# Unread products in TensorE's gaps, and the last expert's rows gathered earlier, in a kernel of attention and two expert layers

## The chip, the core and the metric

One core of a Trainium2 chip. TensorE (PE) multiplies matrices into PSUM; its weights go in by a load of their own (PEld). VectorE (DVE) and ScalarE (ACT) do elementwise work and read PSUM; GpSimd (POOL) works on SBUF alone and issues the gathers and scatters (indirect DMAs); SyncE (SP) issues the plain loads. The metric is the device time of the whole launch in microseconds (us).

## What is computed

Three stages, each on the output of the one before; numpy, cut:

```
# 1: attention, 4 batches, 8 heads, 768 positions, 64 wide: window of 96 and 8 global keys
x = attention(q, k, v).reshape(3072, 512)
# 2: first expert layer: tokens with x @ w_skip > 0, each to its best of 8 experts
e_idx = argmax(xc @ w_gate); gate = softmax(xc @ w_gate)[e_idx]
out[do_compute] = xc + gate * (relu(xc @ w1[e]) @ w2[e])        # w1 512x1024, w2 1024x512
# 3: second expert layer: pairs (token, expert) in order of falling logit;
#    a token goes to the first expert with room, 384 tokens for each of 8
out[mask_e] = relu(x[mask_e] @ w1[e]) @ w2[e]
```

## The kernel before, in words

**Precision.** The experts' products run in fp32r with both operands split in a high and a low part, three products for each (`P3`). A weight chunk of 128x1024 is loaded into `wr`, ACT writes its high part `wh`, and POOL (four pieces of 256 columns) or DVE (one piece) the low part `wl`. `W_.pump()` loads and splits the next chunk if its turn has come; `need(chunk)` splits up to that chunk. Four `wr` buffers are in use: a load waits until the chunk four places earlier is split.

**First layer.** After attention, the routing (`route1`) makes lists of rows (`gid`, `sid`). While it does so, `ww(n)` multiplies parts of two experts' w2 with the next layer's gate; it runs up to the end of that stage. A loop over overflow blocks follows, which here runs zero times; every engine passes its exit. Then come the units, one for each expert, of up to 208 rows: `x_load` gathers the rows (`xg`), `x_stream` transposes them on PE (bank `pt`) into `xh` on ACT and `xl` on DVE, `mm1` makes `ph`, which ACT turns into h (relu) and DVE into its low half, and `mm2_turned` makes `py`. Between the sixth and the seventh expert an extra unit (`extra`, `extra_rest`) handles one overflow block of 128 rows: two halves of `ph<-wh,th`, four transposes for each half, 24 products `py<-wh,th`. The two last experts run `mm1` first and their second products later; they are read with tiles named `py` of 128 and 80 rows, while the second layer's routing goes on.

**Second layer.** The routing (`routing`, `phase`) finds for one expert after the other the threshold that fills it: seven rounds of comparing (`gm` on DVE), counting (`pr<-oh,gm` on PE), deciding (`fl`, `wt`). Then `slots` makes the row list: `ttb`, `part`, `mp` are its small products. Eight units of 384 rows follow; the next expert's routing runs among their products.

**Order.** The program is written by one planner that keeps a model clock for each engine (`ck.at`, `ck.ready`, constants such as 0.19 us between engines). Streams (rows to transpose, routing, the extra unit) hand out steps; `hook` takes a step ahead of a product if the model says that its inputs are ready, `wait_for` steps streams until a condition holds. What stands in the program then runs in that order on each engine. `ck.late` is what the model adds to a gather's 2.7 us until it has landed.

Of the kernel before, what the change touches and what calls it, by code (L numbers as in the profile page):

```python
# [7 lines left out]
F32 = mybir.dt.float32  # L8
# [155 lines left out]
def tile_attn_moe_moe(ctx: ExitStack, tc: tile.TileContext, q, k, v, n_global, n_local,  # L164
                      w_skip, w_gate, w1, w2, w2_gate, w21, w22, out):
    nc = Chip(tc.nc)
# [366 lines left out]
    WWT, WWN = 1, (2, 5)  # L533
    T_GAP, T_SP, T_EPS, T_W, T_P, T_L, T_F, X_B, T_H, T_M, LEAN, T_G, DIRECT, CUT = 0, 0.65, 0.1, 0, 8, 1, 0.3, 3, -4, 0, 2, 1, 13, 16
    T_LOW = 0.7
    ck.late = 2.0
    W_ = Weights()

# [208 lines left out]
        return product  # L747

    ww_todo, ww_turns, ww_k = [], [], [0]

    def ww(n):
        for _ in range(n):
            late = list(ww_turns)
            ww_turns.clear()
            if ww_k[0] < 2 * FC:
                ww_todo.append(ww_step(ww_k[0]))
                ww_k[0] += 1
            if len(ww_todo) > 1 or ww_k[0] == 2 * FC and ww_todo:
                ww_todo.pop(0)()
            for f in late:  # L760
                f()
# [107 lines left out]
    def x_load(U_, nb):  # L869
        U_.xs, U_.xt, U_.at, U_.tb = [], {}, ck.at["pe"], 0  # L870
        ids = U_.ids()
        for tb in range(nb):
            n = U_.n[tb]
            if U_.third:
                xg = ff.tile([128, Dm + E], F32, name=f"xt{tb}", bufs=1)
            elif tb < 2:
                xg = xp.tile([128, Dm + E], F32, name=f"xg{tb}", bufs=2)
            else:
                xg = ff.tile([128, Dm], F32, name=f"xg{tb}", bufs=2)
            gather(xg[:n, :U_.src.shape[1]], U_.src, ids[:n, tb:tb + 1])  # L880
            U_.xs.append(xg)
# [71 lines left out]
    nc.vector.memset(cnt, 2.0)  # L953
    over_rest = over_list(rp, ps, "x", 1.0, gidx, sidx, gwtx, "pP", 5)
    while ww_k[0] < 2 * FC:
        ww(1)
    over_rest()
    while ww_todo or ww_turns:
        ww(1)
    att.close()  # L960
    n_units = nc.values_load(novi[0:1, E:E + 1], min_val=0, max_val=N // 128)
    with tc.For_i(0, n_units, 1):
# [189 lines left out]
    def need(chunk):  # L1152
        while chunk not in W_.parts:
            b4 = W_.split
            W_.pump(True)
            assert W_.split > b4
# [38 lines left out]
            else:  # L1195
                return

    def wait_for(over):
        while not over():
            t = min(s_.when() for s_ in order()) + T_F  # L1200
            s_ = next(s_ for s_ in order() if s_.when() <= t)
            if unit_no[0] < 0 and s_.kind == "main":
                first_ = min((o for o in order() if o.kind != "main"), key=lambda o: o.when(), default=None)
                if first_ and first_.when() < s_.when() + T_M:
                    s_ = first_
            s_.step()

    lows = []
# [339 lines left out]
    def extra(U_, finish):  # L1548

        if U_.g == NE - 1:  # L1550
            X_.xt = {}
            X_.xs = [fx_.tile([128, Dm + E], F32, name="xgx")]
            X_.xh, X_.xl = (fx_.tile([128, KC, 128], F32R, name=n) for n in ("th0", "tl0"))
            gather(X_.xs[0], xd, gidx)
            start("extra", x_stream(X_))
        if U_.g != NE + 1:
            return False
        wait_for(lambda: X_.tb == 1)
        W_.done, W_.f = NE, 0
        need(NE * NCH + 3)  # L1560
        hs_ = []
        for half in range(2):
            ph = fps.tile([128, 512], F32, name="ph", bufs=2)
            xx = (X_.xh, X_.xl)
            for i, (a, b_) in enumerate(P3):
                for c in range(KC):
                    w_ = W_.parts[NE * NCH + c][b_]
                    hook(w_)
                    nc.tensor.matmul(ph, xx[a][:, c, :128], w_[:, half * 512:(half + 1) * 512],
                                     start=i == 0 and c == 0, stop=c == KC - 1 and i == 2)  # L1570
            h2 = ff.tile([128, 2, wide_h], F32, name="h2", bufs=3)
            for i in range(2):
                hs_.append(h2[:, i])
                nc.scalar.activation(hs_[-1], ph[:, i * wide_h:(i + 1) * wide_h], AF.Relu)
            if half == 0:
                finish()
            W_.pump()
            W_.pump()
        start("extra", extra_rest(hs_))
        return True  # L1580

    def extra_rest(hs_):
        hT = []
        for half in range(2):
            yield "pt", hs_[2 * half:2 * half + 2]
            flush()
            p = turns()
            for c in range(4):
                nc.tensor.transpose(p[:, c], hs_[2 * half + c // 2][:, c % 2 * 128:(c % 2 + 1) * 128], ident)
            th = fx_.tile([128, 4, 128], F32R, name=f"th{half}")  # L1590
            tl_ = fx_.tile([128, 4, 128], F32R, name=f"tl{half}")
            nc.scalar.activation(th, p, AF.Copy)
            nc.vector.tensor_tensor(tl_, p, th.bitcast(F32), op=OP.subtract)
            hT.append((th, tl_))
            X_.turned += 1
        X_.y = [fps.tile([128, Dm], F32, name="py2")]
        for c in range(FC):
            need(NE * NCH + 4 + c // 2)
            ww = W_.parts[NE * NCH + 4 + c // 2]
            for i, (a, b_) in enumerate(P3):  # L1600
                yield "pe", [hT[c // 4][a], ww[b_]]
                nc.tensor.matmul(X_.y[0], hT[c // 4][a][:, c % 4], ww[b_][:, (c % 2) * Dm:(c % 2 + 1) * Dm],
                                 start=c == 0 and i == 0, stop=c == FC - 1 and i == 2)
            W_.free = 4 * NE + (c + 1) // 2
            W_.pump()
        epi1(X_, [])
        yield from gate_rows(X_, 1)
# [16 lines left out]
    for tb in range(HI):  # L1624
        x_low(units1[0], tb)
    need(NCH - 3)
    run_units(units1, HI, epi1, (), between)


# [233 lines left out]
    for U_ in units1[NE:]:  # L1863
# [10 lines left out]
            W_.pump()  # L1874
        for tb in range(HI):
            row_late(U_, tb)
    wait_for(lambda: 0 in result)
    f1x.close()
    ff = ctx.enter_context(tc.tile_pool(name="ff", bufs=2))
    width = wide_h = CAP  # L1880
# [18 lines left out]
    def last_blocks(U_, steps):  # L1899

        need(U_.g * NCH + NCH - 1)
        for tb in range(NH):
            for _, f, h in steps:
                ww = W_.parts[U_.g * NCH + 4 + f // 2]
                for i, (a, b_) in enumerate(P3):
                    te(U_.y[tb], h[a][:, tb * 128:(tb + 1) * 128], ww[b_][:, (f % 2) * Dm:(f % 2 + 1) * Dm],
                       start=False, stop=f == FC - 1 and i == 2)
            o = ff.tile([128, Dm], F32, name=f"o{tb}", bufs=1)
            nc.scalar.activation(o[:, :Dm // 2], U_.y[tb][:, :Dm // 2], AF.Copy)
            dv.tensor_copy(o[:, Dm // 2:], U_.y[tb][:, Dm // 2:])  # L1910
            put(U_, tb, o)

    units2 = []
# [18 lines left out]
    def split_next():  # L1932
        need(W_.order[W_.split])

    split_next()
    ck.late = 0
    units2[0].banks = ("pt", "py1", "py2")
    units2[0].load()
    ck.late = 2.0
    split_next()  # L1940
    split_next()
    wait_for(lambda: units2[0].tb == NH)
    split_next()
    W_.on_pool = range(NCH)

    run_units(units2, NH, epi2, by_block=last_blocks)
# [34 lines left out]
```

## Time and profile before

| | us |
|---|---|
| runs | 794.14, 795.55, 795.29, median 795.29 |
| the profiled execution, its own time | 796.18 |
| its span | 794.4 |
| PE busy | 744.9 (94%) |
| DVE, ACT, POOL busy | 528.7, 402.4, 461.6 |

Times of rows count from the start of the span. A row of the timeline reads: start, duration, engine, line, operation, output <- inputs, shapes, how many merged, and in brackets the engine's idle time ahead of it and what ended it. Helpers record every operation, so that all stand at L125. Products are pipelined: the spacing of two rows tells more than their durations. [...]

### The profile page before, as it was taken

How to read it: one execution, taken by the hardware profiler on the slowest of the kernel's cores; microseconds unless marked ns; L12 is line 12 of the kernel's file. 1: busy time of each engine (PE TensorE's matmuls, PEld its weight loads, DVE VectorE, ACT ScalarE, POOL GpSimd, SP SyncE). 2: the span in 40 equal slices, each digit the busy share in tenths (PEclk: the TensorE clock that was granted, in tenths of full speed). 3: DMA queues.
4: the chain of work that ended last, by engine and by line, in shares of the span. 5: the costliest groups of instructions: out<-in, count | busy, mean ns of one | idle time of the engine just before them, and what ended most of it. 6: DMA issues, size and time to landing. Idle time of an engine off the chain costs nothing.

```text
span 794.4 us, 17216 instructions
## 1 busy us (share of the span) xinstructions
PE 744.9 (94%) x5807; PEld 626.9 (79%) x5807; DVE 528.7 (67%) x1953; ACT 402.4 (51%) x934; POOL 461.6 (58%) x807
## 2 busy tenths in 40 slices
PE   6999999999979899999889949999999999999997
PEld 4887777777659899999778627888887888789986
DVE  5987979979456676666643576878787787832111
ACT  5887787887546555555642213343442435345221
POOL 4664556755123474665552635696876859599711
PEclk9999999999989999999989977999999999999999
DMA  8686888988617766668650061536263636466210
GB/s 188 173 209 177 228 225 197 249 200 220 190 48 264 211 200 210 218 218 250 198 198 7 18 212 62 162 104 225 96 213 124 181 125 192 135 184 186 80 41 40
DMA packets 143833, 132.21 MB, mean 166 GB/s; under 512 B 65427, under 2 KB 110739, under 8 KB 143744
## 3 DMA queue, kind: packets, MB, share of 16 engines
q1 hardware_dynamic: 135360, 111.19, 48.9%
q0 software_dynamic: 6784, 19.51, 7.1%
q8 instruction: 47, 0.77, 0.4%
q10 hardware_dynamic: 1600, 0.39, 0.2%
q14 instruction: 42, 0.34, 0.1%
HBM read 108.80 MB, written 22.79 MB: 166 GB/s over the span
## 4 chain that ended last, share of the span: by engine, by line
PE 42%; POOL 11%; issue 8%; DVE 5%; ACT 2%; DMA 2%; POOLq 0%; DVEq 0%; ACTq 0%
PE ph L125 19%; PE py L125 18%; POOL wl L125 8%; PE pr L125 4%; PE pt L125 2%; DVE wl L125 1%; POOL out_dram L125 1%; ACT wh L125 1%; POOL xg L125 1%; DVE py L125 1%; DMA xg<-xd,gid 1%; DMA wr<-in_moe_w_dram 1%; DMA xg<-x2d,ids 0%; DVE h L125 0%; ACT h L125 0%
## 5 line engine op out<-in xcount | busy, mean ns | idle before, releaser
L125 POOL TENSOR_TENSOR wl<-wr,wh 128x256 fp32r<-128x256 f32 x340 | 246.0, 756 | 77.2 <-ACT wh L125 76.5
L125 ACT ACTIVATE wh<-wr 128x1024 fp32r<-128x1024 f32 (+1 forms) x148 | 141.4, 985 | 41.3 <-DMA wr<-in_moe_w_dram 23.3
L125 PE MATMUL py<-wh,h 128*128 128x512 f32 (+1 forms) x448 | 156.6, 405 | 0.0
L125 ACT ACTIVATE h<-ph 128x208 fp32r<-128x208 f32 (+2 forms) x132 | 54.8, 416 | 189.5 <-PE ph L125 173.4
L125 POOL TENSOR_SCALAR pb<-pb,st 128x232 f32<-128x232 f32 (+1 forms) x192 | 83.9, 458 | 73.3 <-ACT pb L125 25.2
L125 DVE SCALAR_TENSOR_TENSOR h<-ph,h 128x208 fp32r<-128x208 f32 (+1 forms) x128 | 58.9, 460 | 101.4 <-ACT h L125 101.0
L125 ACT ACTIVATE pb<-sb,st 128x232 f32<-128x232 f32 (+1 forms) x192 | 113.8, 663 | 10.2 <-DVE st L125 9.6
L125 PE MATMUL ph<-xh,wh 128*128 128x208 f32 (+1 forms) x512 | 103.5, 317 | 4.1 <-DVE h L125 2.2
L125 PE MATMUL ph<-xh,wl 128*128 128x208 f32 (+1 forms) x512 | 103.5, 316 | 0.0
L125 PE MATMUL ph<-xl,wh 128*128 128x208 f32 (+1 forms) x512 | 101.2, 316 | 0.0
L125 PEld LDWEIGHTS ph<-xh,wh 128*128 128x128 f32 x512 | 84.8, 194 | 11.0 <-DVE h L125 2.9
L125 PEld LDWEIGHTS py<-wh,h 128*128 128x128 f32 (+1 forms) x448 | 81.4, 186 | 14.1
L125 PE MATMUL py<-wl,h 128*128 128x512 f32 (+1 forms) x224 | 90.6, 405 | 0.0
L125 PEld LDWEIGHTS ph<-xl,wh 128*128 128x128 f32 x512 | 81.5, 195 | 1.4 <-issue 1.0
L125 PEld LDWEIGHTS ph<-xh,wl 128*128 128x128 f32 x512 | 81.7, 195 | 0.6 <-issue 0.4
L125 DVE TENSOR_TENSOR wl<-wr,wh 128x1024 fp32r<-128x1024 f32 x51 | 64.7, 1276 | 20.2 <-ACT wh L125 20.2
L125 DVE CUSTOM_DVE_ANT_0 sb<-pS,bias 128x232 f32<-128x232 f32 (+1 forms) x192 | 61.4, 374 | 7.9 <-PE pS L125 6.5
L125 DVE COPY pts<-pP 116x512 f32<-116x512 f32 (+1 forms) x96 | 60.6, 672 | 7.5 <-PE pP L125 7.1
L125 POOL DMA_INDIRECT xg<-x2d,ids x24 | 23.3, 970 | 49.4 <-DVE py L125 25.4
L125 PE MATMUL pP<-ident,pb 128*116 128x128 f32 (+1 forms) x384 | 51.1, 276 | 0.0
L125 PE MATMUL pS<-kt,qt 64*128 64x232 f32 (+1 forms) x384 | 49.5, 377 | 1.0 <-ACT pb L125 1.0
L125 PE MATMUL py<-h,wh 128*128 128x416 f32 x192 | 47.9, 363 | 2.4 <-DVE h L125 2.4
(460 smaller groups left out, 1243.4 us busy)
## 6 DMA issues: line engine op xcount, KB each, us to landing
wr<-in_moe_w_dram SPq DMA_DIRECT2D x136, 512.0 KB
xd<-xs SPq DMA_DIRECT2D x32, 192.0 KB
x2d<-xs SPq DMA_DIRECT2D x32, 192.0 KB
kraw<-in_k_dram SPq DMA_DIRECT2D x30, 192.0 KB
qraw<-in_q_dram SPq DMA_DIRECT2D x30, 192.0 KB
vw<-in_v_dram SPq DMA_DIRECT2D x32, 160.0 KB
vw<-in_v_dram SPq DMA_DIRECT2D x32, 120.0 KB
xT<-in_moe_w_dram SPq DMA_DIRECT2D x1, 1536.0 KB
```

The lines of the kernel that those rows point to most:

```text
L125: r = f(*a, **k)
```

## The change

Unread products ("fillers": 128 x 256 columns of the constants `ones` and `tri`, into a PSUM bank that nobody reads) are put on PE in three places: in the last calls of `ww` and ahead of the loop (9, 6 and 6), behind the first unit's transposes (8), and, by `wait_for(..., True)`, up to 0.15 us ahead of each step that the planner expects between the layers (106). The eighth expert's rows (`units1[E - 1]`) are gathered as the extra unit begins, and two pumps move ahead of the extra unit's products; the stream that transposes those rows starts in `extra_rest`. For the second layer's first gathers the planner's `ck.late` is 1.7 where it was 0. The last output blocks are copied by ACT alone.

```
@@ -533,6 +533,7 @@
     WWT, WWN = 1, (2, 5)
     T_GAP, T_SP, T_EPS, T_W, T_P, T_L, T_F, X_B, T_H, T_M, LEAN, T_G, DIRECT, CUT = 0, 0.65, 0.1, 0, 8, 1, 0.3, 3, -4, 0, 2, 1, 13, 16
     T_LOW = 0.7
+    T_U = 0.15
     ck.late = 2.0
     W_ = Weights()
 
@@ -747,14 +748,23 @@
         return product
 
     ww_todo, ww_turns, ww_k = [], [], [0]
-
-    def ww(n):
+    wide_one = ones[:, None, :].to_broadcast([128, 2, 128])
+
+    def keep(n):
+
+        if n:
+            p = ps.tile([128, 512], F32, name="pO")
+            for _ in range(n):
+                nc.tensor.matmul(p[:, :256].rearrange("p (a n) -> p a n", a=2), tri, wide_one, start=True, stop=True)
+
+    def ww(n, unread=0):
         for _ in range(n):
             late = list(ww_turns)
             ww_turns.clear()
             if ww_k[0] < 2 * FC:
                 ww_todo.append(ww_step(ww_k[0]))
                 ww_k[0] += 1
+            keep(unread)
             if len(ww_todo) > 1 or ww_k[0] == 2 * FC and ww_todo:
                 ww_todo.pop(0)()
             for f in late:
@@ -953,10 +963,11 @@
     nc.vector.memset(cnt, 2.0)
     over_rest = over_list(rp, ps, "x", 1.0, gidx, sidx, gwtx, "pP", 5)
     while ww_k[0] < 2 * FC:
-        ww(1)
+        ww(1, 9 if ww_k[0] == 2 * FC - 1 else 0)
     over_rest()
     while ww_todo or ww_turns:
-        ww(1)
+        ww(1, 6 if ww_turns else 0)
+    keep(6)
     att.close()
     n_units = nc.values_load(novi[0:1, E:E + 1], min_val=0, max_val=N // 128)
     with tc.For_i(0, n_units, 1):
@@ -1195,7 +1206,14 @@
             else:
                 return
 
-    def wait_for(over):
+    def warm(until):
+
+        if ck.at["pe"] + 0.11 <= until:
+            p = fps.tile([128, 512], F32, name="ph", bufs=2)
+            while ck.at["pe"] + 0.11 <= until:
+                nc.tensor.matmul(p[:, :256].rearrange("p (a n) -> p a n", a=2), tri, wide_one, start=True, stop=True)
+
+    def wait_for(over, fill=False):
         while not over():
             t = min(s_.when() for s_ in order()) + T_F
             s_ = next(s_ for s_ in order() if s_.when() <= t)
@@ -1203,6 +1221,8 @@
                 first_ = min((o for o in order() if o.kind != "main"), key=lambda o: o.when(), default=None)
                 if first_ and first_.when() < s_.when() + T_M:
                     s_ = first_
+            if fill and s_.need[0] != "dve":
+                warm(s_.when() - T_U)
             s_.step()
 
     lows = []
@@ -1558,6 +1578,10 @@
         wait_for(lambda: X_.tb == 1)
         W_.done, W_.f = NE, 0
         need(NE * NCH + 3)
+        V_ = units1[E - 1]
+        x_load(V_, HI)
+        W_.pump()
+        W_.pump()
         hs_ = []
         for half in range(2):
             ph = fps.tile([128, 512], F32, name="ph", bufs=2)
@@ -1575,7 +1599,6 @@
             if half == 0:
                 finish()
             W_.pump()
-            W_.pump()
         start("extra", extra_rest(hs_))
         return True
 
@@ -1593,6 +1616,7 @@
             nc.vector.tensor_tensor(tl_, p, th.bitcast(F32), op=OP.subtract)
             hT.append((th, tl_))
             X_.turned += 1
+        start("x", x_stream(units1[E - 1]))
         X_.y = [fps.tile([128, Dm], F32, name="py2")]
         for c in range(FC):
             need(NE * NCH + 4 + c // 2)
@@ -1624,6 +1648,7 @@
     for tb in range(HI):
         x_low(units1[0], tb)
     need(NCH - 3)
+    warm(ck.ready("pe", (), [units1[0].xh]) - T_U)
     run_units(units1, HI, epi1, (), between)
 
 
@@ -1874,7 +1899,7 @@
             W_.pump()
         for tb in range(HI):
             row_late(U_, tb)
-    wait_for(lambda: 0 in result)
+    wait_for(lambda: 0 in result, True)
     f1x.close()
     ff = ctx.enter_context(tc.tile_pool(name="ff", bufs=2))
     width = wide_h = CAP
@@ -1906,8 +1931,7 @@
                     te(U_.y[tb], h[a][:, tb * 128:(tb + 1) * 128], ww[b_][:, (f % 2) * Dm:(f % 2 + 1) * Dm],
                        start=False, stop=f == FC - 1 and i == 2)
             o = ff.tile([128, Dm], F32, name=f"o{tb}", bufs=1)
-            nc.scalar.activation(o[:, :Dm // 2], U_.y[tb][:, :Dm // 2], AF.Copy)
-            dv.tensor_copy(o[:, Dm // 2:], U_.y[tb][:, Dm // 2:])
+            nc.scalar.activation(o, U_.y[tb], AF.Copy)
             put(U_, tb, o)
 
     units2 = []
@@ -1933,14 +1957,15 @@
         need(W_.order[W_.split])
 
     split_next()
-    ck.late = 0
+    ck.late = 1.7
     units2[0].banks = ("pt", "py1", "py2")
     units2[0].load()
     ck.late = 2.0
     split_next()
     split_next()
-    wait_for(lambda: units2[0].tb == NH)
+    wait_for(lambda: units2[0].tb == NH, True)
     split_next()
+    warm(ck.ready("pe", (), [units2[0].xh]) - T_U)
     W_.on_pool = range(NCH)
 
     run_units(units2, NH, epi2, by_block=last_blocks)
```

POOL, from the extra unit's weight splits on; `xg <-xd,gid` are the eighth expert's rows, the scatters to `x2d` and `l2d` those of the sixth. Before:

```order
L125 TENSOR_TENSOR wl<-wr,wh 128x256 x8
L125 MEMSET spacer 1x1
L125 DMA x2d<-o_6547,sid 3072x512
L125 MEMSET spacer 1x1
L125 DMA x2d<-o_6566,sid 3072x512
L125 MEMSET spacer 1x1
L125 DMA l2d<-lgo,sid 3072x8
L125 MEMSET spacer 1x1
L125 DMA l2d<-lgo,sid 3072x8
L125 DMA xg_6607<-xd,gid 128x520
L125 DMA xg_6609<-xd,gid 80x520
L125 TENSOR_TENSOR wl<-wr,wh 128x256 x4
```

After:

```order
L125 TENSOR_TENSOR wl<-wr,wh 128x256 x4
L125 DMA xg_6493<-xd,gid 128x520
L125 DMA xg_6495<-xd,gid 80x520
L125 TENSOR_TENSOR wl<-wr,wh 128x256 x4
L125 MEMSET spacer 1x1
L125 DMA x2d<-o_6581,sid 3072x512
L125 MEMSET spacer 1x1
L125 DMA x2d<-o_6595,sid 3072x512
L125 MEMSET spacer 1x1
L125 DMA l2d<-lgo,sid 3072x8
L125 MEMSET spacer 1x1
L125 DMA l2d<-lgo,sid 3072x8
```

The two gathers have moved from behind the second chunk's split and four scatters to ahead of both.

ACT in the same stretch; `h` of 256 columns is the extra unit's, `h` of 208 the seventh expert's, `ya` the sixth expert's epilogue. Before:

```order
L125 ACTIVATE h_6448<-ph 128x208
L125 ACTIVATE h_6473<-ph 128x256 x2
L125 ACTIVATE ya<-py_6184 128x208
L125 ACTIVATE ya<-py_6185 128x208
L125 ACTIVATE ya<-py_6186 128x208
L125 ACTIVATE ya<-py_6187 128x208
L125 ACTIVATE wh<-wr 128x1024 x2
L125 ACTIVATE h_6520<-ph 128x256 x2
```

After:

```order
L125 ACTIVATE h_6481<-ph 128x208
L125 ACTIVATE wh<-wr 128x1024
L125 ACTIVATE wh<-wr 128x1024
L125 ACTIVATE h_6520<-ph 128x256
L125 ACTIVATE h_6520<-ph 128x256
L125 ACTIVATE ya<-py_6217 128x208
L125 ACTIVATE ya<-py_6218 128x208
L125 ACTIVATE ya<-py_6219 128x208
L125 ACTIVATE ya<-py_6220 128x208
L125 ACTIVATE wh<-wr 128x1024
```

Two conversions stand ahead of the first half's relu, and one instead of two behind the epilogue.

PE between the layers: round one of the second expert's routing (24 products `pr<-oh,gm`, of which one row stands here, then `fl,wt`) and the transposes of the second layer's first rows. Before:

```order
L125 MATMUL pt<-tb_rhs,mp 128x27
L125 MATMUL pt<-ident,xg_7558 128x128 x4
L125 LDWEIGHTS gm
L125 MATMUL pr<-oh,gm 32x8
...
L125 MATMUL py_7628<-ident,xg_7560 128x128 x4
L125 LDWEIGHTS wt
L125 MATMUL pr<-fl,wt 128x8
```

After, from the last of the 24 on:

```order
L125 MATMUL pr<-oh,gm 32x8
L125 LDWEIGHTS tri
L125 MATMUL ph<-ones,tri 128x256
...
L125 LDWEIGHTS wt
L125 MATMUL pr<-fl,wt 128x8
...
L125 MATMUL pt<-ident,xg_7618 128x128 x4
```

Round one is now ahead of the transposes; ahead of its 24 products stand 58 fillers, behind them 2 and, after `fl,wt`, 3.

## Rows read from the trace of the kernel before

**Rows 1.** Page, section 2: TensorE's granted clock in 40 equal slices, in tenths.

```profile
PEclk9999999999989999999989977999999999999999
```

**Rows 2.** Stages: length, busy us (count) of PE, PEld, DVE, ACT, POOL; PEclk; DMA share; GB/s.

```profile
231.00:241.20 10.20, 8.01 (x36) 7.63 (x37) 5.62 (x8) 5.52 (x9) 2.98 (x4) 0.50 0.46 135
...
384.00:408.40 24.40, 18.77 (x131) 15.79 (x131) 17.10 (x24) 14.00 (x23) 16.38 (x22) 1.00 0.73 245
408.40:415.30 6.90, 6.72 (x36) 5.90 (x36) 2.40 (x4) 2.46 (x5) 3.05 (x4) 0.51 0.50 192
...
475.50:487.00 11.50, 10.48 (x104) 7.92 (x105) 7.28 (x24) 2.74 (x4) 5.26 (x8) 0.50 0.40 125
...
488.00:789.00 301.00, 300.75 (x1789) 254.00 (x1788) 182.45 (x743) 114.35 (x168) 211.98 (x308) 1.00 0.43 136
```

**Rows 3.** Timeline of PE ahead of and in the first unit.

```profile
232.66 1.65 PE L125 MATMUL py<-ident,xg 128*128 128x128 f32 x8 [2.19 <-DVEq L962]
234.84 1.18 PE L125 MATMUL ph<-xh,wh 128*128 128x208 f32 x4 [0.53 <-ACT xh L125]
235.82 1.05 PE L125 MATMUL ph<-xl,wh 128*128 128x208 f32 x4
236.67 1.05 PE L125 MATMUL ph<-xh,wl 128*128 128x208 f32 x4
...
240.08 0.93 PE L125 MATMUL py<-h,wh 128*128 128x416 f32 x2
...
242.26 0.61 PE L125 MATMUL ph<-xh,wh 128*128 128x208 f32 x4
242.70 0.61 PE L125 MATMUL ph<-xl,wh 128*128 128x208 f32 x4
```

**Rows 4.** Timeline of DVE in the same stretch.

```profile
235.76 2.36 DVE L125 TENSOR_TENSOR wl<-wr,wh 128x1024 fp32r<-128x1024 f32 x2 [0.23 <-ACT wh L125]
...
238.14 0.37 DVE L125 SCALAR_TENSOR_TENSOR h<-ph,h 128x208 fp32r<-128x208 f32 x1
```

**Rows 5.** Timeline of PE from the extra unit on.

```profile
401.17 0.63 PE L125 MATMUL pt<-ident,xg 128*128 128x128 f32 x4 [1.14 <-DMA xg<-xd,gid]
...
408.25 1.03 PE L125 MATMUL ph<-xh,wh 128*128 128x208 f32 x4 [1.81 <-DVE h L125]
...
417.92 0.68 PE L125 MATMUL ph<-xh,wh 128*128 128x208 f32 x4
```

**Rows 6.** Timeline of POOL in that stretch.

```profile
386.64 2.88 POOL L125 TENSOR_TENSOR wl<-wr,wh 128x256 fp32r<-128x256 f32 x4 [7.98 <-ACT wh L125]
...
397.81 4.87 POOL L125 TENSOR_TENSOR wl<-wr,wh 128x256 fp32r<-128x256 f32 x4
```

**Rows 7.** Timeline of ACT in that stretch.

```profile
380.02 0.66 ACT L125 ACTIVATE h<-ph 128x256 f32<-128x256 f32 x2 [3.65 <-PE ph L125]
...
406.50 1.06 ACT L125 ACTIVATE wh<-wr 128x1024 fp32r<-128x1024 f32 x1 [2.72 <-DMA wr<-in_moe_w_dram]
```

**Rows 8.** Timeline of PE between the layers.

```profile
466.68 0.26 PE L125 MATMUL pt<-tb_rhs,mp 128*128 128x27 bf16 x3 [2.46 <-DVE mp L125]
...
475.51 1.09 PE L125 MATMUL pt<-ident,xg 128*128 128x128 f32 x4 [8.57 <-DMA xg<-x2d,ids]
...
476.53 0.80 PE L125 MATMUL pr<-oh,gm 128*32 128x8 bf16 x24
...
481.44 1.33 PE L125 MATMUL ph<-xh,wh 128*128 128x384 f32 x3
```

**Rows 9.** Timeline of DVE between the layers.

```profile
472.48 1.02 DVE L125 TENSOR_TENSOR gm<-m,py 128x512 bf16<-128x512 f32 x2
```

**Rows 10.** Timeline of all engines at the end of the span: ACT and DVE.

```profile
789.13 0.38 ACT L125 ACTIVATE o<-py 128x256 f32<-128x256 f32 x1 [2.40 <-PE py L125]
789.54 0.42 DVE L125 COPY o<-py 128x256 f32<-128x256 f32 x1 [2.36 <-ACT o L125]
```

**Rows 11.** Groups by form, ACT: count | busy us, mean ns | idle ahead.

```profile
L125 ACT ACTIVATE o<-py 128x512 f32<-128x512 f32 x21 | 12.6, 599 | 5.0 <-PE py L125 4.2
```

More of the change, by code (lines that the diff above doesn't have):

```diff
@@ L535, in tile_attn_moe_moe @@
     T_LOW = 0.7
+    T_U = 0.15
     ck.late = 2.0
@@ L749, in tile_attn_moe_moe, with keep, ww @@
     ww_todo, ww_turns, ww_k = [], [], [0]
-    def ww(n):
+    wide_one = ones[:, None, :].to_broadcast([128, 2, 128])
+    def keep(n):
+        if n:
+            p = ps.tile([128, 512], F32, name="pO")
+            for _ in range(n):
+                nc.tensor.matmul(p[:, :256].rearrange("p (a n) -> p a n", a=2), tri, wide_one, start=True, stop=True)
+    def ww(n, unread=0):
         for _ in range(n):
@@ L757, in ww @@
                 ww_k[0] += 1
+            keep(unread)
             if len(ww_todo) > 1 or ww_k[0] == 2 * FC and ww_todo:
@@ L955, in tile_attn_moe_moe @@
     while ww_k[0] < 2 * FC:
-        ww(1)
+        ww(1, 9 if ww_k[0] == 2 * FC - 1 else 0)
     over_rest()
     while ww_todo or ww_turns:
-        ww(1)
+        ww(1, 6 if ww_turns else 0)
+    keep(6)
     att.close()
@@ L1196, in hook, with warm, wait_for @@
                 return
-    def wait_for(over):
+    def warm(until):
+        if ck.at["pe"] + 0.11 <= until:
+            p = fps.tile([128, 512], F32, name="ph", bufs=2)
+            while ck.at["pe"] + 0.11 <= until:
+                nc.tensor.matmul(p[:, :256].rearrange("p (a n) -> p a n", a=2), tri, wide_one, start=True, stop=True)
+    def wait_for(over, fill=False):
         while not over():
@@ L1205, in wait_for @@
                     s_ = first_
+            if fill and s_.need[0] != "dve":
+                warm(s_.when() - T_U)
             s_.step()
@@ L1560, in extra @@
         need(NE * NCH + 3)
+        V_ = units1[E - 1]
+        x_load(V_, HI)
+        W_.pump()
+        W_.pump()
         hs_ = []
@@ L1577, in extra @@
             W_.pump()
-            W_.pump()
         start("extra", extra_rest(hs_))
@@ L1595, in extra_rest @@
             X_.turned += 1
+        start("x", x_stream(units1[E - 1]))
         X_.y = [fps.tile([128, Dm], F32, name="py2")]
@@ L1626, in tile_attn_moe_moe @@
     need(NCH - 3)
+    warm(ck.ready("pe", (), [units1[0].xh]) - T_U)
     run_units(units1, HI, epi1, (), between)
@@ L1876, in tile_attn_moe_moe @@
             row_late(U_, tb)
-    wait_for(lambda: 0 in result)
+    wait_for(lambda: 0 in result, True)
     f1x.close()
@@ L1908, in last_blocks @@
             o = ff.tile([128, Dm], F32, name=f"o{tb}", bufs=1)
-            nc.scalar.activation(o[:, :Dm // 2], U_.y[tb][:, :Dm // 2], AF.Copy)
-            dv.tensor_copy(o[:, Dm // 2:], U_.y[tb][:, Dm // 2:])
+            nc.scalar.activation(o, U_.y[tb], AF.Copy)
             put(U_, tb, o)
@@ L1935, in tile_attn_moe_moe @@
     split_next()
-    ck.late = 0
+    ck.late = 1.7
     units2[0].banks = ("pt", "py1", "py2")
@@ L1941, in tile_attn_moe_moe @@
     split_next()
-    wait_for(lambda: units2[0].tb == NH)
+    wait_for(lambda: units2[0].tb == NH, True)
     split_next()
+    warm(ck.ready("pe", (), [units2[0].xh]) - T_U)
     W_.on_pool = range(NCH)
```

## The prediction, made before the changed kernel had run

> **What bounds the kernel now.** I read the page's slices first: TensorE (PE) is busy in nearly all of them, and its granted clock is full except in a few [rows 1]. Then I cut the span into stages and read busy time and clock of each [rows 2]. [...] From 488 to 789 us PE is busy for 300.75 of 301 us at clock 1.00, so whatever starts that stretch earlier ends the kernel earlier. [...]
>
> **1. Ahead of the first unit.** Now: the eight transposes of the first rows start at 232.66 after 2.19 us of idle, the first hidden product (ph) at 234.84, groups of four spaced 0.85 us (235.82 to 236.67), and six groups end at 240.08 [rows 3]. At full clock such groups are 0.44 us apart (242.26 to 242.70) [rows 3], so six take 2.65 us where they take 5.24 now: at most 2.6 us.
>
> Not all of it arrives. The first py product reads the low half of h, which VectorE (DVE) makes behind two weight splits; those end at 238.12, h runs from 238.14 for 0.37 us [rows 4]. With PE faster h is waiting for its input no longer, but DVE is no earlier: py can start at about 238.6 and not at 240.08. Gain 1.5 us.
>
> The added fillers: 9, 6 and 6 unread products of 256 columns ahead of the loop, 8 behind the transposes. No row has this shape. Its price is between the 0.11 us spacing of the 208-column products (0.44 over four [rows 3]) and that scaled by columns, 0.14; I take 0.12, and double at the lower clock. The last 6 (0.7 us) stand between PE's last product and its passage through the loop's exit. If the 2.19 us of idle is PE's own walk, they cost up to 0.7 us; if it waits for DVE, as the row says, nothing. I take 0.5, and the transposes win back as much by running at full clock (1.65 us for eight now). The 8 take 1.0 us where 0.53 us was idle: about 0.2 late, which the DVE chain covers. Bounds for this place: +1.9 (no cost) and −0.9 (the clock falls anyway and the fillers run at half rate: 8 × 0.24 less 0.53 is 1.4, plus 0.5, less the 1 us that DVE's lateness hides).
>
> Between 242 and 384 the order of instructions is unchanged and PE is nearly gapless, so I carry the 1.5 us through; bounds 0 and all of it.
>
> **2. The extra unit.** From 384.0 to 408.4 PE is busy 18.77 of 24.4 us: 5.6 us idle. From 408.4 to 415.3 it is busy 6.72 us at 0.51, of which half, 3.3 us, is the price of the lower clock [rows 2]. Together 9.0 us. The largest idle pieces are 1.14 us for the gathered rows xg at 401.17 and 1.81 us at 408.25 [rows 5].
>
> - The rows. The two gathers stand on GpSimd (POOL) behind four scatters. Now POOL meets them in the 7.98 us that it idles ahead of its split at 386.64 [rows 6]. No extra instruction; the scatters behind them (read only in the second layer) are later by about 2.6 us, which nothing near waits for.
> - Two pumps move ahead of the extra unit's products: two weight conversions go to the 3.65 us in which ScalarE (ACT) idles ahead of 380.02 [rows 7]. The same number of pumps follows. The whole chain of loads, which frees its buffers by these splits, moves up by some 5 us.
> - The 1.81 us at 408.25: ACT's relu of h stood behind a conversion that waited 2.72 us for its load, to 406.50 [rows 7]. That load waits for a buffer, freed by POOL's split at 397.81, which came late behind scatters and gathers and took 4.87 us instead of 2.88 [rows 6]. The gathers are out of its way now, the scatters are not.
>
> With the waits gone nothing lets the clock fall there. I leave 1.5 us for a conversion that still waits with a relu behind it (bounds 0 and 3), and 0.8 us for transposes that wait for the single bank pt, since they now follow each other more closely. Gain 9.0 − 2.3 = 6.7 us. Bounds: 9.0, and 3.0 (the 1.81 us stays, the rest of the 5.6 goes but for the 0.8, and the clock falls as before).
>
> [...]
>
> **3. Between the layers.** PE's last useful products before the second layer end with mp at 466.68; it then idles 8.57 us until the first rows x land (475.51) [rows 8]. Round 1 of the routing has its input ready at 473.50 (DVE gm, 472.48 + 1.02 [rows 9]), but its products stand behind that transpose. In the new order they stand ahead of it, after 58 fillers: 58 × 0.12 = 7.0 us from 466.94, that is 473.9; bounds 473.3 and 475.1 by the prices above. So round 1 is about 2.6 us earlier. Rounds are a chain through PE and DVE of about 3 us; three of them now stand ahead of the unit's first product where two stood. That product thus starts at about 481.6, against 481.44 now [rows 8], but with one more round done (0.9 us of PE) and at full clock. Now 5.56 us pass from 481.44 to 487.0 at 0.50 [rows 2]; less a round's 0.85, 4.7 us are unit products, and half of them, 2.3 us, comes back. Less 0.2 for the start and 0.6 for waits that the quicker PE meets: 2.3 + 0.9 − 0.8 = 2.4 us. Bounds +3.5 and −7 (rival C).
>
> The landing of the rows is not moved: POOL's gather and its scatters keep their order. The other 29 fillers there stand in gaps (19 in the 2.46 us ahead of mp [rows 8]).
>
> **4. The end.** The last output block leaves PSUM by half a copy on ACT (0.38 us from 789.13) and half on DVE, one after the other, to 789.96 [rows 10]; one copy of 512 columns on ACT takes 0.599 [rows 11], to 789.73. Gain 0.2 us; bounds 0 and 0.3. In the second layer the order of routing pieces among products is re-dealt; at 300.75 of 301 busy I cost it 0, bounds ±1.
>
> **The sum.** 1.5 + 6.7 + 2.4 + 0.2 = 10.8 us. The profiled execution took 796.18 us, so it would take 785.4; it stands 0.9 above the median of the runs, 795.29, and on that basis I forecast 784.5 us.
>
> **Rivals.**
> A. The clock falls ahead of the first unit in spite of the fillers, since some 2 us without any product and eight transposes lie between them. For: it is low now from 231.0 on [rows 2], with the 2.19 us of idle behind that [rows 3], of which at least 1.4 us stays. Against: 29 fillers are added. Place 1 then gives −0.9: 784.5 + 2.4 = 786.9 us.
> [...]
> B. At the extra unit the rows are early, but ACT still meets a late load with a relu behind it, PE stands as long, and the clock falls again. For: the load chain through POOL keeps its scatters. Against: it starts 5 us earlier. Place 2 gives 3.0: 788.2 us.
> C. Slower: unread products do not hold the clock, and they then run at half rate in front of useful work. At place 3, 19 × 0.24 = 4.6 us puts mp some 2 us late and 58 × 0.24 = 13.9 us the first round at about 483 instead of 476.5; the unit starts after three slow rounds: −7 with one round won back. With −0.9 at place 1: −0.9 + 6.7 − 7 + 0.2 = −1.0, that is 796.3 us; it is slower by over 0.2% once place 2 gives less than 6.1. Against: in the stretches where PE is full of products the clock is 1.00 throughout.
>
> **The numbers.** Forecast 0.5; A 0.2; B 0.15; A and B together 0.05 (790.6); C 0.1. A measurement here can tell about 0.2%, 1.6 us. Of C's ten in a hundred, four lie within that and six are slower; with one more for mishaps in the re-dealt second layer I say faster 0.89, same 0.04, slower 0.07. The range runs from the forecast's upper bounds nearly added (1.9 + 9.0 + 3.5 + 0.3 = 14.7, so 780.6) to A and B together: 780.5 to 791.
>
> **What would show it.** Place 1: clock 1.00 from 230 to 242, the first ph at about 235, first py at 238.6. Place 2: xg gathered ahead of the split that stood at 386.64, the extra unit's py products uninterrupted, clock 1.00, the last unit's first ph about 8 us earlier than 417.92 [rows 5]. Place 3: clock 1.00 from 463 on, round 1's products ahead of the first transposes of x. End: one ACT copy of 0.6 us. I am wrong if fillers run at 0.2 us or more, or if PE stands as long at the extra unit, waiting for ACT.

## The result and the profile after

The changed kernel takes 786.25 us (median of 787.59, 785.89, 786.04 and 786.46) where the kernel before, on the same chip, takes 795.38: a ratio of 0.9883, 95% interval 0.9858 to 0.9907. The forecast was 784.5, within 780.5 to 791. The profiled execution took 787.59 us, with a span of 785.8.

First the page's slices, TensorE's granted clock in tenths of full speed. The two sevens and two eights of before [rows 1] are gone:

```profile
PEclk9999999999999999999999999999999999999999
```

Then the stages of the changed kernel (columns as in [rows 2]; PEclk is the granted clock as a share of full speed):

```profile
230.00:234.00 4.00, 1.93 (x16) 1.27 (x14) 0.86 (x5) 0.81 (x2) 0.17 (x1) 1.00 0.03 6
234.20:237.70 3.50, 3.50 (x19) 3.04 (x20) 1.71 (x3) 2.57 (x4) 1.50 (x2) 0.51 0.44 124
268.40:271.80 3.40, 3.40 (x17) 3.38 (x17) 3.06 (x8) 1.12 (x2) 3.40 (x4) 0.50 0.59 164
401.50:404.90 3.40, 3.40 (x18) 3.40 (x18) 2.65 (x5) 1.29 (x2) 1.56 (x2) 0.50 0.91 267
...
463.00:480.00 17.00, 15.09 (x189) 11.85 (x186) 13.14 (x39) 3.79 (x5) 8.50 (x11) 1.00 0.51 167
480.00:781.00 301.00, 300.49 (x1791) 254.25 (x1789) 181.03 (x739) 115.30 (x169) 211.75 (x308) 1.00 0.42 139
```

Between the layers the clock stays at 1.00 in this execution. At the start of the first layer and behind the extra unit it still falls, for 3.4 us where it was low for 10.2 and 6.9 [rows 2], and at 268.4 there is a low stretch that the kernel before did not have.

**Place 1**, PE's timeline, which answers to [rows 3]:

```profile
231.12 0.82 PE L125 MATMUL pO<-ones,tri 128*128 128x256 bf16 x6
234.08 1.54 PE L125 MATMUL py<-ident,xg 128*128 128x128 f32 x8 [2.14 <-issue]
235.42 1.91 PE L125 MATMUL ph<-ones,tri 128*128 128x256 bf16 x8
236.98 0.99 PE L125 MATMUL ph<-xh,wh 128*128 128x208 f32 x4
...
240.04 0.56 PE L125 MATMUL py<-h,wh 128*128 128x416 f32 x2
...
267.27 1.03 PE L125 MATMUL py<-h,wh 128*128 128x416 f32 x4 [2.01 <-DVE h L125]
```

The idle ahead of the transposes is as long as before, 2.14 us, and the clock falls in spite of the fillers. The first py stands at 240.04, 30.01 us behind the first `pS<-w2t,wg`, against 30.65 before. An idle of 2.01 us stands ahead of the second low stretch; before, the first of these waits was 0.81:

```profile
265.67 1.02 PE L125 MATMUL py<-h,wh 128*128 128x416 f32 x4 [0.81 <-DVE h L125]
```

**Place 2**, PE, then POOL, then DVE (compare [rows 5] and [rows 6]):

```profile
378.48 0.85 PE L125 MATMUL ph<-wh,th 128*128 128x512 f32 x3
...
394.89 0.60 PE L125 MATMUL pt<-ident,xg 128*128 128x128 f32 x4
...
400.88 0.70 PE L125 MATMUL ph<-xh,wh 128*128 128x208 f32 x4 [1.77 <-DVE h L125]
```

```profile
381.26 1.82 POOL L125 DMA_INDIRECT xg<-xd,gid  x1
...
395.98 2.82 POOL L125 TENSOR_TENSOR wl<-wr,wh 128x256 fp32r<-128x256 f32 x4
```

```profile
398.15 1.73 DVE L125 TENSOR_TENSOR wl<-wr,wh 128x1024 fp32r<-128x1024 f32 x1 [1.31 <-POOL wl L125]
399.81 0.74 DVE L125 SCALAR_TENSOR_TENSOR o<-py,gwtx,xgx 128x512 f32<-128x512 f32 x1
400.47 0.36 DVE L125 SCALAR_TENSOR_TENSOR h<-ph,h 128x208 fp32r<-128x208 f32 x1
```

The rows are gathered in POOL's idle time and transposed without a wait. One wait stays, 1.77 us at 400.88: DVE's h, which frees the ph bank, stands behind a weight split and an output block.

**Place 3**, PE, then POOL, and ACT at the end (compare [rows 8] and [rows 10]):

```profile
461.06 0.24 PE L125 MATMUL pt<-tb_rhs,mp 128*128 128x27 bf16 x3 [0.36 <-DVE mp L125]
461.15 6.49 PE L125 MATMUL ph<-ones,tri 128*128 128x256 bf16 x58
467.60 0.76 PE L125 MATMUL pr<-oh,gm 128*32 128x8 bf16 x24
...
470.72 0.66 PE L125 MATMUL pt<-ident,xg 128*128 128x128 f32 x4 [1.50 <-DMA xg<-x2d,ids]
...
476.20 0.76 PE L125 MATMUL ph<-xh,wh 128*128 128x384 f32 x3
```

```profile
459.72 0.92 POOL L125 DMA_INDIRECT x2d<-o,sid  x1 [6.82 <-DVE fx L125]
466.21 1.00 POOL L125 DMA_INDIRECT xg<-x2d,ids  x1 [5.57 <-DVE py L125]
```

```profile
780.79 0.60 ACT L125 ACTIVATE o<-py 128x512 f32<-128x512 f32 x1 [2.19 <-PE py L125]
```

**Where the time went.** The spans differ by 8.6 us (794.4 and 785.8). PE's timeline cuts this into five parts, by the starts of the same rows in both:

| from, to | before | after | change |
|---|---|---|---|
| start to first `pS<-w2t,wg` (ahead of every filler) | 209.43 | 210.03 | +0.60 |
| to the extra unit's first `ph<-wh,th` | 167.61 | 168.46 | +0.85 |
| to the first mp | 89.64 | 82.58 | −7.06 |
| to the last product | 322.02 | 319.30 | −2.72 |
| to the end of the span | 5.71 | 5.45 | −0.26 |

The first part is the difference of two executions and not of the change (the first `pS<-w2t,wg` starts at 209.1 to 211.0 in all profiles). Place 1 lost 0.85 us, the other three gained 10.0.

### The profile page after: what moved, and what is told of

Same layout as the page of the kernel before. It is cut to its first block, busy times and chain, and to the rows that moved or that the text cites. A ratio compares the mean times of both kernels' runs of the same rounds, so it can differ in the third digit from the quotient of the medians.

```text
span 785.8 us, 17475 instructions
## 1 busy us (share of the span) xinstructions
PE 752.7 (96%) x5942; PEld 635.8 (81%) x5942; DVE 529.5 (67%) x1950; ACT 403.0 (51%) x934; POOL 463.2 (59%) x807
## 4 chain that ended last, share of the span: by engine, by line
PE 51%; issue 6%; POOL 5%; DVE 4%; DMA 3%; ACT 1%; POOLq 0%; ACTq 0%; DVEq 0%
PE ph L125 23%; PE py L125 22%; PE pr L125 3%; POOL wl L125 3%; PE pt L125 2%; DMA wr<-in_moe_w_dram 2%; DVE wl L125 1%; ACT wh L125 1%; POOL out_dram L125 1%; DMA xg<-x2d,ids 1%; DVE py L125 0%; POOL x2d L125 0%; POOL xt L125 0%; DVE xl L125 0%; DVE o L125 0%
## 5 line engine op out<-in xcount | busy, mean ns | idle before, releaser
L125 PE MATMUL ph<-xh,wh 128*128 128x208 f32 (+1 forms) x512 | 100.5, 313 | 1.8 <-DVE h L125 1.8
L125 PE MATMUL ph<-xh,wl 128*128 128x208 f32 (+1 forms) x512 | 101.1, 313 | 0.0
L125 PE MATMUL ph<-xl,wh 128*128 128x208 f32 (+1 forms) x512 | 99.4, 313 | 0.0
L125 PEld LDWEIGHTS ph<-xh,wh 128*128 128x128 f32 x512 | 83.2, 192 | 7.1 <-DVE h L125 1.9
L125 PE MATMUL pO<-pts,vw 116*64 116x128 f32 x640 | 46.3, 281 | 4.0 <-DVE pts L125 2.6
```

The costliest lines, as they stand in the source:

```text
L125: r = f(*a, **k)
```

## The experiments

Each kernel ran five rounds beside the kernel before. The intervals are about ±0.3%, wider than the 0.2% of the prediction and too wide for parts of 1 or 2 us, so the ratios stand beside stage lengths of the profiled executions. The columns: A, from the first `pS<-w2t,wg` to the third expert's first product; B, from the extra unit's first product to mp; C, from mp to the second layer's first product; D, from there to PE's last product. "Low" lists where the clock stood at 0.50 or 0.51, 3.4 us each if no length is given; stretches in the first 20 us and from PE's last product on are left out. (For before, [rows 2] show the end of the last one: it begins at 466.5.) Fillers are read by nobody, so all kernels compute the whole.

| kernel | ratio (95%) | low from | A | B | C | D |
|---|---|---|---|---|---|---|
| before | | 231.0 (10.2), 408.4 (6.9), 466.5 (20.5) | 72.86 | 89.64 | 14.76 | 307.26 |
| changed | 0.9883 (0.9858–0.9907) | 234.2, 268.4, 401.5 | 73.69 | 82.58 | 15.14 | 304.16 |
| E1 no exit fillers | 0.9886 (0.9848–0.9924) | 401.7, 470.0 | 70.57 | 82.68 | 16.80 | 304.21 |
| E2 none ahead of first layer | 0.9897 (0.9860–0.9935) | 229.4 (10.2), 403.5, 471.8 | 72.40 | 82.62 | 16.80 | 304.23 |
| E3 none between layers | 0.9887 (0.9850–0.9923) | 233.0, 267.2, 403.7, 461.7 (27.3) | 73.46 | 82.57 | 14.89 | 307.90 |
| E4 extra unit alone | 0.9937 (0.9912–0.9962) | 229.7 (10.2), 403.8, 461.9 (27.3) | 72.38 | 82.49 | 15.17 | 310.07 |
| E5 changed again | 0.9861 (0.9833–0.9889) | 233.6, 400.8 | 72.69 | 82.20 | 14.09 | 304.21 |
| E6 no exit fillers again | 0.9883 (0.9851–0.9916) | 233.6, 400.8 | 72.53 | 82.28 | 14.98 | 304.15 |
| E7 late split | 0.9869 (0.9837–0.9900) | 139.1, 398.5, 466.8 | 70.49 | 82.13 | 17.40 | 304.19 |
| E8 fillers in the wait | 0.9897 (0.9873–0.9922) | 234.5, 268.6, 470.0 | 72.48 | 82.07 | 16.34 | 304.17 |
| E9 no exit, no eight | 0.9888 (0.9858–0.9918) | 233.8 (6.8), 291.9 | 72.43 | 81.68 | 16.05 | 304.46 |
| E10 rows before routing | 0.9907 (0.9875–0.9939) | 233.5, 404.2, 472.5 | 72.55 | 81.36 | 16.53 | 306.05 |
| E11 twenty ahead of mp | 0.9881 (0.9854–0.9908) | 139.3, 402.1 | 70.93 | 84.18 | 13.56 | 306.24 |
| E12 no fillers | 0.9918 (0.9899–0.9937) | 230.2 (10.2), 291.6 (6.8), 404.3, 462.3 (27.3) | 72.57 | 82.63 | 15.31 | 307.86 |

**E1**, the changed kernel without the last six fillers.

```
-    keep(6)
     att.close()
```

> The changed kernel without the last 6 fillers, those between PE's last product and its passage through the loop's exit; all other instructions stand in the same order. Theory (these six delay everything behind the exit by what they take, 0.61 us in the trace, the load chain of the first layer too, and with it come the 2.01 us wait and the second fall of the clock at 268 us): the first transposes stand about 0.6 us earlier against the last product ahead of the loop, the wait near 267 shrinks below 1.7 us, the clock does not fall there; 0.6 to 2.2 us less, 784.0 to 785.7. Rival (the six keep the clock up through the exit, at least in part): without them the clock is low from 231 us on for as long as before the change, 10 us instead of 3.4; 1.7 to 3 us more, 788 to 789.

The clock of E1 at place 1, by stages:

```profile
230.00:234.40 4.40, 2.04 (x20) 1.58 (x18) 0.87 (x3) 1.25 (x4) 1.22 (x2) 1.00 0.02 6
234.40:241.00 6.60, 6.16 (x49) 5.75 (x49) 4.76 (x7) 5.77 (x8) 2.99 (x4) 1.00 0.73 223
```

No fall at all there, although PE idled 2.36 us ahead of the transposes, and A is 3.1 us below that of the changed kernel. That looked like the theory, although the ratio is that of the changed kernel; E6 took it back.

**E2**, no filler ahead of the first layer.

```
-        ww(1, 9 if ww_k[0] == 2 * FC - 1 else 0)
+        ww(1)
-        ww(1, 6 if ww_turns else 0)
-    keep(6)
+        ww(1)
-    warm(ck.ready("pe", (), [units1[0].xh]) - T_U)
```

> The changed kernel without any filler ahead of the first layer (9, 6, 6 and 8); all else in the same order. Theory (the two traces say that this part costs 0.85 us in sum, since what the clock gives at the start, 1.5 us, is lost again by 274 us): the low clock comes back for about 10 us at the start, the first hidden product stands as before the change, no fall at 268 us; 0.5 to 1 us less than the changed kernel, about 785.4. Rival (my forecast: this part is worth 1.5 us, and the loss at 268 us has nothing to do with it): 1.5 us more, about 787.7.

```profile
229.40:239.70 10.30, 7.44 (x34) 6.80 (x35) 4.80 (x9) 5.08 (x9) 1.86 (x2) 0.50 0.29 79
```

The low stretch is back at its full length, and A is 72.40: 1.1 to 1.3 us less than with the fillers and two falls (changed, E3), 1.8 more than with the others and no fall (E1). Neither theory nor rival is right for all executions.

**E3**, no filler between the layers, the order kept.

```
-    wait_for(lambda: 0 in result, True)
+    wait_for(lambda: 0 in result)
-    wait_for(lambda: units2[0].tb == NH, True)
+    wait_for(lambda: units2[0].tb == NH)
-    warm(ck.ready("pe", (), [units2[0].xh]) - T_U)
```

> The changed kernel without the fillers between the layers; the order of all other instructions, with round one of the routing ahead of the transposes, stays. Theory (the fillers hold the clock, the order only moves one round): PE idles as long as before the change between mp and the transposes, the clock is at 0.50 for some 10 us at the start of the second layer, and half of the unit products in it, about 2.3 us, is lost; 788.0 to 789.0. Rival (the order alone gives it, since the clock costs little while PE waits for DVE): within 0.5 us of the changed kernel, 786.3.

```profile
461.70:489.00 27.30, 17.12 (x165) 13.88 (x165) 18.77 (x59) 8.34 (x11) 12.10 (x17) 0.50 0.46 162
```

The clock is low throughout the gap and for 11 us of the second layer, and D is 3.7 us longer than in E1 and E2 on the same chip. C is 1.9 us shorter there, but C goes with the gap between the last scatter and the first gather (5.87 us in E3, 7.70 and 7.33 in E1 and E2), and that gap differs as much between kernels with the same fillers there (last section). The theory holds in kind, by D; the ratios of E1 and E3 (0.9886 and 0.9887) do not tell the two apart.

With the fillers the clock is not always up either. In five of the ten profiles that have them it falls for 3.4 us between the layers (E1, E2, E7, E8, E10), behind idles of 1.4 to 2.4 us that the fillers leave. These are PE and the stage in E1:

```profile
469.81 0.16 PE L125 MATMUL pr<-fl,wt 32*128 32x8 bf16 x1 [1.80 <-issue]
```

```profile
470.00:473.40 3.40, 3.40 (x24) 2.72 (x24) 2.67 (x9) 0.74 (x2) 3.07 (x5) 0.50 0.50 145
```

Each time it is up again before the second layer's first product, and D does not show it: 304.21 in E1, 304.16 in the changed kernel.

**E4**, the kernel before with the edits at the extra unit alone (the three hunks from `V_ = units1[E - 1]` to `start("x", ...)` in the diff above).

> The kernel before with the edits at the extra unit alone (rows gathered and two pumps ahead of its products, the stream started in the rest); no filler anywhere, old tail, old order between the layers. Theory (that part is worth 7.05 us by the two traces, and does not hang on the fillers): 788.3, with the clock still falling for some 3 us behind a wait of ACT near 405 us. Rival (part of it comes from the first layer running at another phase of the load chain): 3 to 5 us less than before, 790 to 792.

B is 82.49, as in the changed kernel: 7.15 us, no filler needed. On this chip the ratio gives 5 us (0.63% of 799.63), with an interval that reaches to 7. The theory holds by the stage, not yet by the ratio. In the profile D takes back 2.8 us (310.07 against 307.26): the second layer's first product comes at 477.6 instead of 481.4, but the low stretch lasts to 489 instead of 487, so the unit's products are slow for 11.5 us instead of 5.5. That would account for the missing 2 us; it rests on one profile of each kernel.

**E5 and E6**, the changed kernel and E1 again, side by side.

> The changed kernel as it is, on the chip on which the three others of this call run, so that they have a baseline. Against the kernel before 0.988, as in the first comparison. Theory of place 1: the clock falls for about 3.4 us as the first unit's transposes begin and again near 267 us behind a wait of 2 us. Rival (the two falls were chance of one execution): neither shows.

> The changed kernel without the last 6 fillers, again, now beside the changed kernel on the same chip. Theory (these six make the whole first layer late and cause the second fall of the clock): from the last product ahead of the loop to the extra unit's first product it takes 2 to 3 us less than in the changed kernel, and the run is 2 to 3 us faster. Rival (phase of the clock, not the six): no difference beyond 0.6 us.

Now both show one fall, at 233.6, and A of 72.69 and 72.53: leaving out the six fillers saves 0.2 us here, not 3. What E1 had shown was the clock that did not fall in that execution. The rival of E6 holds.

**E7**, without the six, and with two pumps fewer at the end of the extra unit.

```
             W_.free = 4 * NE + (c + 1) // 2
-            W_.pump()
+            if c < FC - 2:
+                W_.pump()
```

> As the one without the last 6 fillers, and in the rest of the extra unit the last two of eight pumps are left out, so that one weight conversion (ACT) and one split (DVE) stand behind the h that PE waits for at 400.88 instead of ahead of it. Theory (that wait of 1.77 us, and the 3.4 us of half clock behind it, come from the split of a late load that stands ahead of h): the wait falls below 0.7 us, the clock stays up there, 2 to 3.4 us less than without the pumps' removal. Rival (the two splits now stand together ahead of the next h, and PE waits there instead): the same wait one product group later, no gain beyond 0.5 us.

DVE and then PE in E7:

```profile
395.26 2.36 DVE L125 TENSOR_TENSOR wl<-wr,wh 128x1024 fp32r<-128x1024 f32 x2 [0.63 <-ACT wh L125]
```

```profile
397.96 0.72 PE L125 MATMUL ph<-xh,wh 128*128 128x208 f32 x4 [1.63 <-DVE h L125]
```

The rival: two splits now stand together ahead of the next h, and PE waits there, one group later, for 1.63 us.

**E8**, without the six, and 14 fillers ahead of the group that waits.

```
     def mm1(U_, f, n_tok):
+        if U_.defer == 0 and f == 3:
+            p = fps.tile([128, Dm], F32, name="py1")
+            for _ in range(14):
+                nc.tensor.matmul(..., tri, wide_one, start=True, stop=True)
```

> As the one without the last 6 fillers, and 14 fillers (14 x 0.112 = 1.6 us) on PE ahead of the product group that waits at 400.88. Theory (what counts for the clock is that PE has products, unread ones too): the clock stays at 1.00 behind the wait, its 3.4 us at half rate go, 1.5 us less than without these fillers. Rival (the wait is late by something that the fillers make later, or the clock falls all the same): 0 to 1.6 us more.

PE's timeline of E8, and the stage:

```profile
398.69 1.70 PE L125 MATMUL py<-ones,tri 128*128 128x256 bf16 x14
400.65 0.70 PE L125 MATMUL ph<-xh,wh 128*128 128x208 f32 x4 [0.26 <-DVE h L125]
...
407.20 0.36 PE L125 MATMUL ph<-xh,wh 128*128 128x208 f32 x1 [0.80 <-DVE h L125]
```

```profile
398.70:404.90 6.20, 5.89 (x51) 5.30 (x50) 5.13 (x8) 3.87 (x6) 3.25 (x3) 1.00 0.77 248
```

The clock stays up, as the theory says; one execution does not show that the fillers did it, since in E9 it stayed up at this place without them. B is 82.07 against 82.28 in E6. The quicker PE meets DVE again at 407.20 and waits 0.80 us. The low stretch behind the extra unit cost 0.2 us by this pair, 0.6 by E6 and E9 (81.68), 0.9 by the changed kernel and E9, and not 1.5.

**E9**, without the six and without the eight behind the transposes (both lines as in E1 and E2).

> The changed kernel without the last 6 fillers ahead of the loop's exit and without the 8 behind the first unit's transposes; 9 and 6 and all between the layers stay. Theory (the 8 cost more than the 0.53 us of idle that they fill: 1.56 us at half clock, and buy nothing, since the clock is set by the idle at the exit): the first hidden product stands 0.4 to 1 us nearer to the transposes than in the changed kernel, the clock low for 0 or 3.4 us at the start, no more; the first py as with the 8 or up to 0.3 us earlier; time within 1 us of the changed kernel. Rival (the 8 are what ends the low stretch early): low for 6.8 or 10 us, the first py 0.7 to 1 us later, 1 to 2 us more.

```profile
233.80:240.60 6.80, 6.06 (x28) 5.90 (x28) 5.22 (x7) 5.19 (x8) 1.93 (x4) 0.50 0.61 187
```

The rival: the eight end the low stretch earlier, 3.4 us instead of 6.8. The first py stands 30.35 us behind the first `pS<-w2t,wg`, against 29.33 in E6. Of this 1.0 us nothing is left by the third expert: A is 72.43, and 72.53 in E6.

**E10**, the changed kernel, with no routing step let in among the last products of the first layer.

```
-                hook(U_.h[a][:, f], ww[b_])
+                if U_.g < E or tb < HI - 1 or f < FC - 1:
+                    hook(U_.h[a][:, f], ww[b_])
```

> The changed kernel with the last product block of the first layer's last expert letting no routing step in, so that DVE makes the last 80 output rows (o, 458.70 in the trace) ahead of the routing's go and part; all fillers stay. Theory (what PE waits for between the layers is the gather of the rows, and the gather waits for the landing of the last scatter of output rows, 5.7 us behind its start; round one and mp have slack): o and the scatter start about 1.2 us earlier, the first transposes too, against PE's last product of the layer; 0.8 to 1.2 us less than the changed kernel. Rival (the rows' ids bound the gather, or the routing, which now has go and part behind mp): transposes no earlier, or the first unit product as late as before; 0 to 1 us more.

POOL in E10, the last scatter and the first gather:

```profile
460.08 0.91 POOL L125 DMA_INDIRECT x2d<-o,sid  x1 [5.89 <-DVE fx L125]
...
467.57 1.00 POOL L125 DMA_INDIRECT xg<-x2d,ids  x1 [6.58 <-DVE py L125]
```

The theory fails: the gather follows 7.49 us behind the scatter, against 6.49 in the changed kernel, which takes back what was won, and the planner put two routing rounds instead of three ahead of the first unit product: D is 1.9 us longer.

**E11**, the changed kernel with 20 more fillers ahead of the first mp.

```
         pi = turns()
+        if not ph_:
+            p = fps.tile([128, 512], F32, name="ph", bufs=2)
+            for _ in range(20):
+                nc.tensor.matmul(..., tri, wide_one, start=True, stop=True)
```

> The changed kernel with 20 more fillers (20 x 0.112 = 2.24 us) on PE directly ahead of the first mp, from which the ids of the gathered rows come. Theory (the ids are there 3 us before the last scatter lands, so mp has slack): the gather starts where it did, the first transposes stand where they did against the last scatter, and the planner puts some 20 fewer fillers behind mp; within 0.7 us of the changed kernel. Rival (mp is on the path): everything behind it 2.2 us later, 2 us more.

B is 1.6 us longer and C as much shorter than in the changed kernel (84.18 and 13.56 against 82.58 and 15.14): mp has slack (the first gather starts 4.3 us behind it here, 5.15 in the changed kernel), and the landing of the rows sets the start. Here too only two rounds fit ahead, and D is 306.24. The theory holds for the path, and the round that moved back shows its price.

**E12**, no filler at all (the edits of E2 and E3 together).

> The changed kernel without any filler; the edits at the extra unit, the order between the layers and the tail stay. Theory (the parts measured one by one add up: 7.1 us at the extra unit, 2.4 us for the order between the layers, 0.3 us at the end, and about 0 for the fillers ahead of the first layer; the fillers between the layers bring 1.8 us more, which go here): 9.5 to 10 us faster than the kernel before where the changed kernel is 9 to 11, a ratio of 0.987 to 0.989; clock low for 10 us at the start, 3.4 behind the extra unit and 20 or more between the layers. Rival (the fillers carry a large part, as the forecast's 1.5 and 2.3 us say): 7 us faster, a ratio of 0.991 or more.

The ratio is 0.9918, so the rival, though the intervals overlap: by the ratios the fillers carry 2.8 us of 9.3 (0.9918 less 0.9883, of 795.4), and by E5's ratio, 0.9861, whose interval lies clear of this one, 4.5. My theory had counted 1.8 us for the fillers between the layers; D alone says 3.7 (307.86 against 304.2).

## Why the prediction was right, point by point

**Place 1, forecast +1.5, measured −0.85.** The steps that failed are "clock 1.00 from 230 to 242" and "I carry the 1.5 us through". The size was right: in the profiles in which the clock did not fall there (E1, E7, E11) A is 70.5 to 70.9, and in the four without any filler there (before, E2, E4, E12) 72.4 to 72.9, a gain of 1.5 to 2.4. But it fell once in E5, E6, E9 and E10 (72.4 to 72.7, no gain), and twice in the changed kernel and E3 (73.5 to 73.7) and, without the six, in E8 (72.5). Rival A said that it falls; that its −0.9 is close to what came is luck. It put the loss ahead of the first py, and there the changed kernel was 0.64 us ahead (30.01 against 30.65 us behind the first `pS<-w2t,wg`; 29.78 in E5). The loss came later: where the clock is low for 3.4 us at the start, the wait for h near 266 us lasts 2.0 us (changed, E3, E5, E6, E8, E10), elsewhere 0.8 to 0.9. Why it is longer was not tried. In three of these six (changed, E3, E8) a second fall follows it. The same instructions (changed, E3, E5, E10, E11), with the same idle of 2.1 us at the loop's exit, gave no fall, one and two. Of the fillers, the eight bring the first py 1.0 us forward when the clock has fallen, which A does not keep (E9); the last six cost 0.1 to 1.1 (A with and without them at the same number of falls: 70.93 and 70.53, 72.62 and 72.53, 73.58 and 72.48), and the forecast had 0.5.

Rival A counted the eight transposes with the idle time. In E9 they stand between idles of 2.37 and 0.74 us, and the clock is low for 6.8 us; in E6, with the eight fillers in the place of the 0.74, for 3.4. No run here tries the transposes alone, so what they do to the clock was not shown.

**Place 2, forecast +6.7, measured +7.06.** The gathers met POOL's idle time, and the wait for xg and the one for a conversion (1.23 us ahead of 385.67 in the kernel before) are gone. The wait that I left, 1.5 us, measured 1.77; its cause is DVE's split ahead of h (E7) and not ACT alone. "With the waits gone nothing lets the clock fall there" was wrong, as in rival B, but the fall cost 0.2 to 0.9 us and not half of 3.4 (E8, E9): with the clock up PE waits for DVE again, 0.80 us in E8. So 6.7 came out although its clause on the clock did not. The last unit's first ph came at 412.32, 7.04 us nearer to the extra unit's first product than before, where I said about 8. Rival B's price was for both the wait and the clock in full. POOL's split took 2.82 us where it had taken 4.87 [rows 6]. DVE's, begun at 398.15 while POOL's ran, took 1.73 us, where E7's two took 2.36 together; why it took longer was not tried.

**Place 3, forecast +2.4, measured +2.72.** The clock held at 1.00 in this execution, the fillers took 0.112 us each (6.49 over 58; forecast 0.12), and the first unit product stood 15.14 us behind mp (forecast 14.9: 481.6 less 466.68). So the sum was right, by luck: its two terms were not, and their errors cancel. D tells them apart: 310.07 with the old order and without fillers (E4), 307.9 with the new order alone (E3, E12), 306.1 with fillers and two rounds ahead (E10, E11), 304.2 with both (304.46 in E9). The moved round brings 1.9 to 2.2 us where I took 0.9. The clock brings 3.7 to 3.9 against a low stretch that lasts to 489, and 1.1 (307.26 less 306.15) against the one of the profiled execution of before, where I took 2.3.

**The end, forecast +0.2, measured +0.26.** One copy of 0.60 us.

**The sum.** −0.85 + 7.06 + 2.72 + 0.26 is 9.2 us, where I had 10.8; the start of the program took back 0.6 more in this execution. By E5's ratio, 0.9861, it is 11 us. The executions differ: over E5's six the mean granted clock runs from 0.990 to 0.998, and the one with 0.998 is the fastest, 782.45 us, where the slowest took 786.85. Rival C is excluded: the 58 ran at 0.112 us each, and mp came no later for the fillers ahead of it (B is 82.58 with them and 82.57 without, E3). What I held against it, that the clock is 1.00 where PE is full of products, does not hold everywhere: from 401.5 PE was busy for 3.40 of 3.40 us at 0.50.

## What to carry to other kernels

Fillers paid where they filled nearly all of a long idle time (8.57 us between the layers [rows 8]) behind which useful products ran at a clock of 0.50 without them: 3.7 us by D, although an idle of 1.4 to 2.4 us that was left there still let the clock fall for 3.4 us in five of ten profiles. At a loop's exit, for whose 2.14 us of idle the row of the changed kernel names no other engine, fillers ahead of it and behind it left the clock to chance: no fall (E11), one (E5) or two (changed) with the same instructions. Price such a term as a mix of outcomes. And half a clock was not half of the time: the 3.4 us at 0.50 behind the extra unit cost 0.2 to 0.9 us. So ask first whether the slow products would have waited for another engine anyway. One profile is not enough to credit a clock effect to an edit; E1 looked decisive until E6 ran.

## What the runs showed of the hardware that was not expected

Whether a wait lowers the clock is not settled by its length: 1.78 us at the extra unit did not in E9, where 1.77 did in the changed kernel; 2.36 us at the loop's exit did not in E1 and E7, and did in E8; 2.01 us near 266 did not in E5, and did in the changed kernel. What decides it stays open here. The two that did not, in E9 and in E5:

```profile
402.11 0.70 PE L125 MATMUL ph<-xh,wh 128*128 128x208 f32 x4 [1.78 <-DVE h L125]
```

```profile
265.86 1.03 PE L125 MATMUL py<-h,wh 128*128 128x416 f32 x4 [2.01 <-DVE h L125]
```

In the profiles of E1 to E4 and E9 to E12, and not in the others, one ACT instruction, the same in all eight, starts 3.4 to 3.5 us late, and PE idles 2.1 us behind it. This is its row in E1:

```profile
289.60 0.34 ACT L125 ACTIVATE h<-ph 128x208 fp32r<-128x208 f32 x1 [3.46 <-remote]
```

Nothing in the program releases it, and no run here tells what does. Columns A to D leave this place out. The chip alone does not decide it: E12 ran on the chip of E5 to E8. In E1, E9 and E12 an instruction of DVE's (fl) between the layers starts 2.4 to 2.8 us late in the same way; that lies in column C.

From the start of the last scatter to the first gather it took 5.5 us (E5) to 8.5 (E7) with the same instructions on POOL, and C goes with it: 14.09 and 17.40. In the six profiles whose traces tell when that scatter landed (before, changed, E5 to E8) it lands 4.7 to 7.7 us behind its start, and the gather starts 0.77 or 0.78 us behind the landing in every one, while the row numbers (`ids`) had been ready for 2.6 to 5.6 us. So the gather waits for the scatter, as E10's theory had it. What makes a landing late was not tried.
